# First-layer steps on the scores' PSUM banks: one slot in four, and two banks by turns after the last attention unit

## Chip, cores, metric

One core of a Trainium2 chip. The metric is the device time of one execution in microseconds (us). Before the change it is 310.82 us, the median of 3 runs (310.35 to 310.94).

## What is computed

The reference is sliding-window attention followed by a two-layer network with an ELU between the layers:

```python
# q, k, v: 8 batches, 8 heads, 576 positions, 64 wide
scores = scale * np.matmul(q, k.transpose(0, 1, 3, 2))
mask = (rel >= 0) & (rel < 128)
scores = np.where(mask, scores + bias[None], -1000000000.0)
attn = softmax(scores)                    # along the keys
x = matmul(attn, v)                       # -> 4608 tokens x 512
h = x @ w_in                              # 512 -> 2048
g = np.where(h > 0.0, h, np.exp(np.minimum(h, 0.0)) - 1.0)
out = g @ w_out                           # 2048 -> 512
```

## The kernel before

Everything runs in one hand-written order (the scheduler is off). The order is a list of numbered **slots**. In each slot the kernel issues, in this order: early tasks, one **first-layer step** (`hidden`, L297), the ELU of the step of the slot before (`done`, L531, which calls `elu`, L319), the slot's other tasks, its second-layer products (`product`, L384), and late tasks. Each engine takes its instructions in the order in which they were issued, so a wait in one of them holds back all that stands behind it on that engine.

**A first-layer step.** For a token block `t` of 512 tokens a step makes two chunks of 128 hidden units for 256 tokens, in one PSUM bank of 128 x 512 float32. TensorE runs 8 matmuls of 256 columns (L305; 16 shorter ones where the ring of transposed tokens wraps). ScalarE then reads the bank. In "soft" slots it does both parts of the exponential itself (L312, L313); in the others it does one pass (L315) and GpSimd clamps (L316). VectorE makes the ELU from that and from the bank (L323); this is the bank's last reader. A step is free to overwrite a bank when the ELU that read it last has ended. There are 16 steps for each block; blocks 2 to 8 have slots 38 to 149.

**PSUM.** The kernel uses all eight banks: `spa` (two banks, which are `sp[0]` and `sp[1]`), `sp[2]`, `sp[3]`, `hp[0]`, `hp[1]`, `av` and `op`. From slot 38 on, first-layer steps alternate between `hp[0]` and `hp[1]`, so a step reuses the bank of the step two slots earlier. The products of the second layer use `av` and `op`. For n = 17, the last half block, they use `sp[0]`, `sp[2]` and `sp[3]` instead, from slot 150 on.

**Attention.** Batches 2 to 7 start at the slots 31, 48, 66, 83, 100 and 117 (`START`). A batch has four units of four slots. A unit that starts at slot a does this:

- late in slot a: scores (L225) into `sp[0..3]`, 16 matmuls (32 in the last unit), in turn over the four banks, each on a quarter of the array's rows;
- slot a+1: ScalarE's exp of `spa` (L233), ahead of that slot's first-layer step; then weighing on VectorE (L241);
- slot a+2: ScalarE's exps of `sp[2]` and `sp[3]` (L236), again ahead of the step; then weighing;
- slot a+3: `all_values` (L263): value products into `spa` (L271), then reciprocal and division on VectorE (L276, L277), and a transposing DMA on SP's queue;
- the last unit only, slot a+4: `values` (L243) for the remaining 64 queries, 8 matmuls into `sp[2]` and then 8 into `sp[3]` (L253), with their reciprocals and divisions (L259, L260).

Scores of the next unit are issued late in slot a+4, so `sp[2]` and `sp[3]` have no user between the exps of slot a+2 and those scores (or those last value products). Slot numbers grow by four from unit to unit, and the last scores of batch 7 are in slot 129; its last value products are in slot 133.

**The second layer** computes pairs of 128 x 256 quarters with seven products in place of eight (lines 341 to 418). Its sums of slices of `g` and its combinations run on VectorE (L354) between the ELUs, and its copies on ScalarE (L396, L398). Seven 8-matmul products (L393) are spread over eight slots, so a slot without attention work is 8 first-layer and 7 second-layer matmuls.

The lines that give each step its bank:

```python
BUF = [hp[0], hp[1], sp[2], sp[3]]
for t in range(2, NTB):
    for j in range(16):
        step = (256 * (j // 8), 256, 2 * (j % 8), 2)
        HID[16 * t + 6 + j] = [(t, *step, BUF[(j + 1) % 2])]
```

Of the kernel before, what the change touches and what calls it, by code (L numbers as in the profile page):

```python
# [18 lines left out]
def kernel(  # L19
# [14 lines left out]
    NTB = NTOK // 512  # L34
# [42 lines left out]
    sp = [spa[:, 0, :], spa[:, 1, :]] + [ps_s.tile([128, 512], F32, name=f"sp{i}", tag=f"sp{i}") for i in (2, 3)]  # L77
    hp = [ps_h.tile([128, 512], F32, name=f"hp{i}", tag=f"hp{i}") for i in range(2)]
# [70 lines left out]
    with tc.manual_schedule():  # L149
# [341 lines left out]
        early, tasks, late, HID, OUT = {}, {}, {}, {}, {}  # L491

        def at(s, f, *a):
            tasks.setdefault(s, []).append((f, a))
# [4 lines left out]
        def after(s, f, *a):  # L499
            late.setdefault(s, []).append((f, a))  # L500
# [4 lines left out]
        BUF = [hp[0], hp[1], sp[2], sp[3]]  # L505
# [6 lines left out]
        steps += [(1, c0, 128, 4 * f, 4) for c0 in (256, 384) for f in range(4)]  # L512
        for s, step in enumerate(steps):
            HID[s if s < 18 else s + 6] = [(*step, (hp[0], hp[1], av, hp[1])[s] if s < 4 else BUF[(s + 1) % (3 if s < 18 else 2)])]
        for t in range(2, NTB):
            for j in range(16):
                step = (256 * (j // 8), 256, 2 * (j % 8), 2)
                HID[16 * t + 6 + j] = [(t, *step, BUF[(j + 1) % 2])]
        SEVEN = range(1, 18)

        XY = {1: (op, sp[3]), 2: (op, av)}
# [2 lines left out]
        for o in range(16 * NTB):  # L524
            t, ts, f = o // 16, o // 4 % 4, o % 4
            if o // 8 in SEVEN:
                continue
            s = (9, 11, 13, 14)[o] if o < 4 else 11 + o if o < 13 else 2 * o - 1 if o < 16 else 15 + o
# [62 lines left out]
        at(31, values, 1, 4, 1)  # L591
        at(32, turn, 1, 4)


        START = [None, None, 31, 48, 66, 83, 100, 117]

        TURN = [None, None, (22, 24, 25, 28), (35, 39, 43, 47)]
        REST = 32, 33, 36, 37
        for b in range(2, B):
            for u in range(4):  # L600
                a = START[b] + 4 * u
                after(a, scores, b, u)
# [6 lines left out]
                if u == 3:  # L609
                    at(a + 4, values, b, 4, 0, sp[2])  # L610
                    at(a + 4, values, b, 4, 1, sp[3])
                    at(a + 4, turn, b, 4)
            a = START[b - 1] if b > 2 else 0
            for n in range(4):
# [16 lines left out]
        for n in SEVEN:  # L631
            s = 15 + 8 * n
# [66 lines left out]
```

The softmax here doesn't subtract the row's maximum and nothing guards it: scores larger than these inputs give would overflow.

## Time and profile before

| | |
|---|---|
| Timed runs, median of 3 | 310.82 us (310.35 to 310.94) |
| Profiled execution, first to last instruction | 308.9 us |
| Granted TensorE clock, mean | 0.998 |
| Busy: TensorE matmul / VectorE / ScalarE / GpSimd | 300.1 / 257.5 / 241.8 / 108.4 us |
| L305, first-layer matmuls into hp | 1488, busy 144.2 us |
| L323, ELU, 128 x 512 | 679 ns each |
| L312 + L313, soft step on ScalarE | 597 + 631 ns each |
| L225, scores of batches 2 to 7 | first at 71.3 us, last at 264.5 us |

A row of the profile's groups names the line, the engine, the operation, what it writes and reads, the shape and the count; then the busy time, the mean of one in ns, and the idle time of the engine ahead of it with its releaser. In the timeline a row gives the start and the length in us of one instruction, or of a run of like ones ("x8"). TensorE's matmuls are pipelined, and their ends are modelled: rows of one run overlap, so an idle time between two ends says less than the distance between two starts.

Two views serve for what follows: the page, and the timeline of all engines in a few microseconds. The first-layer step of a slot is found in the timeline as a run of L305 on TensorE; its ELU is the L323 that belongs to it in order.

### The profile page before, as it was taken

To read this page: it belongs to the slowest core of one execution; us is meant where nothing else is said; L and a number is where in the kernel's file an instruction comes from. 1 tells how busy PE (TensorE), PEld (TensorE's weight loads), DVE (VectorE), ACT (ScalarE), POOL (GpSimd) and SP (SyncE) were. 2 spreads that over 40 slices of the span, in tenths; PEclk is the share of its full clock that TensorE was granted. 3 is DMA by queue.
4 is the path that set the end of the run, shared out by engine and by line. 5 is a ranking of instruction groups with operands and counts; after the bars stand their busy time and mean duration, and the time that the engine had idled before them with its cause. 6 is when DMAs were issued, how large, how long until landed. Compare 5 with 4: busy or idle time off the path is not lost.

```text
span 308.9 us, 9820 instructions
## 1 busy us (share of the span) xinstructions
PE 300.1 (97%) x4071; PEld 256.1 (83%) x4071; DVE 257.5 (83%) x498; ACT 241.8 (78%) x446; POOL 108.4 (35%) x163
## 2 busy tenths in 40 slices
PE   6899999999999999999999999999999999999995
PEld 4788875798888888988888888888899888898884
DVE  4646888988989998997989998989998788886782
ACT  4576678678798788878887889778888897968871
POOL 8937867273252315141616061706000001010000
PEclk9999999999999999999999999999999999999999
DMA  9999999999194919395969896999530202030103
GB/s 96 196 197 202 201 180 185 94 118 115 21 165 63 169 35 161 43 152 59 132 70 138 110 102 78 138 124 122 60 94 7 91 17 87 19 98 0 70 28 110
DMA packets 96509, 32.04 MB, mean 104 GB/s; under 512 B 83920, under 2 KB 91984, under 8 KB 96464
## 3 DMA queue, kind: packets, MB, share of 16 engines
q0 software_dynamic: 75920, 18.36, 64.2%
q1 hardware_dynamic: 20400, 12.98, 17.1%
q8 instruction: 32, 0.52, 0.7%
q14 instruction: 13, 0.11, 0.1%
q10 hardware_dynamic: 144, 0.07, 0.1%
HBM read 36.70 MB, written 9.44 MB: 149 GB/s over the span
## 4 chain that ended last, share of the span: by engine, by line
PE 72%; DVE 8%; DMA 6%; ACT 5%; POOL 4%; issue 4%; POOLq 0%; DVEq 0%
PE hp L305 33%; PE op L393 13%; PE av L393 12%; DMA VP<-in_v_dram 4%; PE spa L225 3%; PE spa L271 3%; DVE g L323 3%; POOL e L316 2%; PE sp L393 2%; ACT e L315 2%; DMA s<-in_q_dram 2%; ACT EX L236 1%; PE sp L253 1%; POOL VP L114 1%; DVE xn L260 1%
## 5 line engine op out<-in xcount | busy, mean ns | idle before, releaser
L305 PE MATMUL hp<-xT,wi 128*128 128x256 f16 (+3 forms) x1488 | 144.2, 245 | 1.0 <-DVE g L323 0.5
L305 PEld LDWEIGHTS <-wi 128*128 128x128 f16 x1600 | 119.9, 98 | 18.1 <-issue 6.3
L323 DVE SCALAR_TENSOR_TENSOR g<-e,hp 128x512 f16<-128x512 f32 x138 | 93.7, 679 | 22.2 <-ACT e L313 12.5
L316 POOL TENSOR_SCALAR e<-e 128x512 f32<-128x512 f32 x44 | 28.0, 636 | 158.8 <-ACT e L315 152.9
L312 ACT ACTIVATE e<-hp 128x512 f32<-128x512 f32 x98 | 58.6, 597 | 28.5 <-PE hp L305 23.1
L313 ACT ACTIVATE e<-e 128x512 f32<-128x512 f32 x100 | 63.1, 631 | 3.2
L393 PEld LDWEIGHTS <-S 128*128 128x128 f16 x544 | 51.2, 98 | 6.7 <-issue 0.6
L393 PEld LDWEIGHTS <-g 128*128 128x128 f16 x408 | 38.2, 98 | 4.7 <-issue 0.6
L241 DVE TENSOR_TENSOR EX<-EX,TAB 128x1024 f16<-128x1024 f16 x48 | 32.9, 686 | 6.2 <-ACT EX L236 4.0
L114 POOL DMA_DIRECT2D VP<-in_v_dram x40 | 34.6, 878 | 0.6 <-PE hp L305 0.3
L315 ACT ACTIVATE e<-hp 128x512 f32<-128x512 f32 x40 | 24.1, 601 | 10.9 <-PE hp L305 10.9
L393 PE MATMUL op<-T,S 128*128 128x256 f16 x200 | 30.0, 273 | 0.1
L233 ACT ACTIVATE EX<-spa 128x1024 f16<-128x1024 f32 x24 | 24.6, 1025 | 3.7 <-PE spa L225 3.4
L393 PE MATMUL av<-T,S 128*128 128x256 f16 x176 | 26.4, 273 | 0.1
L236 ACT ACTIVATE EX<-sp 128x512 f16<-128x512 f32 x48 | 26.0, 596 | 0.0
L354 DVE TENSOR_TENSOR S<-g 128x1024 f16<-128x1024 f16 (+2 forms) x35 | 23.5, 671 | 0.8 <-PE op L393 0.2
L393 PE MATMUL op<-wo,g 128*128 128x256 f16 x128 | 19.2, 272 | 0.1
L393 PE MATMUL av<-wo,g 128*128 128x256 f16 x120 | 18.0, 272 | 0.0
L277 DVE TENSOR_TENSOR xn<-spa,rden 128x512 f16<-128x512 f32 x24 | 16.6, 692 | 0.8
L108 POOL DMA_DIRECT2D st<-in_k_dram x24 | 16.2, 686 | 2.8 <-DMA s<-in_q_dram 1.9
L108 POOL DMA_DIRECT2D st<-in_q_dram x24 | 15.9, 666 | 0.6 <-DMA VP<-in_v_dram 0.6
L271 PE MATMUL spa<-VP,EX 128*128 128x65 f16 x336 | 15.4, 193 | 0.1
(139 smaller groups left out, 379.3 us busy)
## 6 DMA issues: line engine op xcount, KB each, us to landing
out_dram<-ob SPq DMA_DIRECT2D x35, 256.0 KB, 2.2
VP<-in_v_dram POOLq DMA_DIRECT2D x32, 128.0 KB, 5.7
st<-in_k_dram POOLq DMA_DIRECT2D x24, 144.0 KB, 5.2
st<-in_q_dram POOLq DMA_DIRECT2D x24, 144.0 KB, 5.9
wi<-in_moe_w_in_dram POOLq DMA_DIRECT2D x4, 512.0 KB, 10.7
wo<-in_moe_w_out_dram POOLq DMA_DIRECT2D x4, 512.0 KB, 10.1
VP<-in_v_dram POOLq DMA_DIRECT2D x8, 64.0 KB, 5.8
s<-in_k_dram POOLq DMA_DIRECT2D x1, 512.0 KB, 12.1
```

The costliest lines, as they stand in the source:

```text
L108: nc.gpsimd.dma_start(st[b][32 * g:32 * g + 32, w, :, :, :, :].rearrange("p h n j d -> p (h n) (j d)"), (q, k)[w][b, 2 * g:2 * g + 2, :, : ...
L114: nc.gpsimd.dma_start(VP[b % 2][0:p, n, :, 0:D], v[b, :, 128 * n:128 * n + p, :].rearrange("h p d -> p h d"))
L236: nc.scalar.activation(unit(b, u)[:, g, :, :], sp[g].rearrange("p (h c) -> p h c", h=2), AF.Exp, scale=0.125)
L241: V.tensor_tensor(out=e, in0=e, in1=TAB[:, int(u == 3), 2 * gp:2 * gp + 2, :, :], op=ALU.mult)
L271: nc.tensor.matmul(a[:, h // 4, h % 4, :], ex_[u][:, c:c + 128], VP[b % 2][:, n, h, 0:D + 1], start=j == 0, stop=j == len(parts) - 1)
L305: nc.tensor.matmul(p[:, l * w + u0:l * w + u1], w_in_sb[:, c, fc * 128:(fc + 1) * 128], xT[:, c, x0:x0 + u1 - u0], start=(c == 0), stop=(c ...
L312: nc.scalar.activation(e[:, 0:n], p[:, 0:n], AF.Relu, scale=-1.0)
L313: nc.scalar.activation(e[:, 0:n], e[:, 0:n], AF.Exp, scale=-1.0)
L315: nc.scalar.activation(e[:, 0:n], p[:, 0:n], AF.Exp)
L316: nc.gpsimd.tensor_scalar(out=e[:, 0:n], in0=e[:, 0:n], scalar1=1.0, scalar2=0.0, op0=ALU.min, op1=ALU.max)
L323: V.scalar_tensor_tensor(out=gs[t][:, f0:f0 + nf, c0:c0 + w], in0=sh(es.pop((t, c0, f0))), scalar=1.0, in1=sh(hps.pop((t, c0, f0))), op0=A ...
L393: nc.tensor.matmul(o, a[:, j, :], b[:, j, :], start=j == 0 and i in (1, 2, 5), stop=j == 7, skip_group_check=True)
```

## The change

From slot 38 to 145, first-layer steps no longer all use the two hp banks. In the slot a+3 of each unit of batches 2 to 7 the step's bank is `sp[2]` for the first three units of a batch and `sp[3]` for the fourth. After slot 133 (`ended` is 134) the odd slots use `sp[3]` and `sp[2]` by turns. All other steps take the hp banks by turns, counted over those steps alone. No instruction is added, removed or moved on any engine; the banks, and the waits that follow from them, differ. The list `START` is moved up in the file, so the lines after it have other numbers in the changed kernel.

```diff
+        START = [None, None, 31, 48, 66, 83, 100, 117]
+        spare = {a + 4 * u + 3: sp[2 + u // 3] for a in START[2:] for u in range(4)}
+        ended, full = START[-1] + 17, 0
         for t in range(2, NTB):
             for j in range(16):
+                s = 16 * t + 6 + j
                 step = (256 * (j // 8), 256, 2 * (j % 8), 2)
-                HID[16 * t + 6 + j] = [(t, *step, BUF[(j + 1) % 2])]
+                if s in spare and s < 16 * NTB + 2:
+                    bank = spare[s]
+                elif s >= ended and s < 16 * NTB + 2 and s % 2:
+                    bank = sp[2 + s // 2 % 2]
+                else:
+                    bank, full = hp[(full + 1) % 2], full + 1
+                HID[s] = [(t, *step, bank)]
```

More of the change, by code (lines that the diff above doesn't have):

```diff
@@ L592 @@
         at(32, turn, 1, 4)
-        START = [None, None, 31, 48, 66, 83, 100, 117]
         TURN = [None, None, (22, 24, 25, 28), (35, 39, 43, 47)]
```

## The prediction

> **What bounds the kernel now.** I read the page first (busy shares, chain, groups), then TensorE's own waits, then the timeline, all engines, around one attention unit and around the end of one batch.
>
> ```profile
> PE 300.1 (97%) x4071; PEld 256.1 (83%) x4071; DVE 257.5 (83%) x498; ACT 241.8 (78%) x446; POOL 108.4 (35%) x163
> ...
> PE 72%; DVE 8%; DMA 6%; ACT 5%; POOL 4%; issue 4%; POOLq 0%; DVEq 0%
> ...
> L305 PE MATMUL hp<-xT,wi 128*128 128x256 f16 (+3 forms) x1488 | 144.2, 245 | 1.0 <-DVE g L323 0.5
> ```
>
> TensorE carries 97% of the span and 72% of the chain. The third line books only 0.5 us of waiting for the ELU (L323) to the first layer, but that is idle time between modelled ends, which overlap (245 ns per row). Waits shorter than that show only in the starts. So I went through TensorE's rows by start: a 256-column matmul follows the one before it by 0.109 us (280.44 to 282.08 us holds 15 of them: 1.64), a 65-column one by 0.031. A start later than that is a stall.
>
> The timeline of the last batch (b = 7, third unit) shows both the wait that the change removes and the one that it adds:
>
> ```profile
> 260.09 1.04 PE L305 MATMUL hp<-xT,wi 128*128 128x256 f16 x8
> ...
> 261.55 0.82 PE L393 MATMUL av<-wo,g 128*128 128x256 f16 x6
> 261.57 0.69 DVE L323 SCALAR_TENSOR_TENSOR g<-e,hp 128x512 f16<-128x512 f32 x1 [0.46 <-ACT e L313]
> ...
> 262.18 0.68 DVE L354 TENSOR_TENSOR S<-S,g 128x1024 f16<-128x1024 f16 x1
> 262.31 1.03 PE L305 MATMUL hp<-xT,wi 128*128 128x256 f16 x8
> ...
> 262.78 0.20 DVE L276 RECIPROCAL rden<-spa 128x8 f32<-128x8 f32 x1
> 263.01 0.69 DVE L277 TENSOR_TENSOR xn<-spa,rden 128x512 f16<-128x512 f32 x1
> ...
> 263.62 0.68 DVE L323 SCALAR_TENSOR_TENSOR g<-e,hp 128x512 f16<-128x512 f32 x1
> ...
> 264.04 0.26 PE L225 MATMUL spa<-QT,KT 32*128 32x192 f16 x2
> 264.05 0.26 PE L225 MATMUL sp<-QT,KT 32*128 32x192 f16 x2
> ```
>
> Slot 129's step (262.31) could have started at 261.55 + 6 x 0.109 = 262.21. Its bank is free when the ELU of step 127 ends (261.57 + 0.69 = 262.26). It starts 0.05 after that, so 0.10 is lost; the 0.05 is the same in every such wait.
>
> **Part 1: the waits removed.** In the slots that the change touches (38 to 149) thirteen steps start late for this reason, in us: slot 43 0.13, 46 0.11, 49 0.09, 50 0.23, 70 0.35, 78 0.23, 91 0.13, 94 0.12, 99 0.13, 121 0.24, 125 0.11, 129 0.10, 133 0.11: 2.06 in all. That is the most this part can give. (Another 0.09 at each first step after scores is the change between row shapes and stays.) With one step of four on a scores bank, two of the three steps on hp reuse a bank three slots old and one still two slots old; 49 and 50 are of the latter kind, so 1.74 is removed directly.
>
> **Part 2: two banks by turns from slot 135 on.** The steps from 134 to 149 follow each other by 1.64 us, 15 matmuls x 0.109, with stalls of 0.001 to 0.002: nothing to win. A release that now comes 0.22 us early (2 slots old) will come 3.5 early. Value 0.
>
> **Part 3: the waits added.** No instruction moves on any queue, SP's and POOL's included; only banks and waits differ. A borrowed bank has two new edges. First, the borrowed step (slot a+3 of a unit that starts at slot a) waits for that unit's exp (L236). Second, whoever writes the bank next waits for the borrowed step's ELU: the next unit's scores at the end of slot a+4 for sp[2], and the second half of the batch's last value product (L253) in slot a+16 for sp[3]. Behind the waiting matmul stands all of TensorE's queue: the rest of the scores, hence ScalarE's exps and VectorE's weighing, and the next first-layer step.
>
> In the rows above, step 128's ELU runs 263.62 to 264.30. Scores began at 264.04; they can now write sp[2] only at 264.30 + 0.05 = 264.35: +0.31 against before. The 0.10 saved at slot 129 doesn't lower that, as nothing on the way to this ELU depends on step 129. It is the end of a run on VectorE without a gap: ELU of 127, S, reciprocal, xn, ELU of 128, that is 261.57 to 264.30, started by ScalarE (L313 ends 261.54), which itself worked since the unit's scores. So it is a loop: scores, exps, two ELUs with xn between, scores again. The loop is now longer than TensorE's work between two scores (7.80 us from 256.24 to 264.04, less the stalls), and it repeats after each unit, so the losses add up.
>
> The same sum (ELU end + 0.05 - scores' start, against before, so with part 1 contained) for each unit after the first of a batch: slot 39 +0.03, 43 +0.30, 52 +0.08, 60 +0.13, 70 +0.04 (0.35 saved, 0.39 waited), 78 +0.04, 87 +0.30, 91 +0.30, 95 +0.10, 108 +0.20, 121 +0.31, 125 -0.11 (ELU early enough, the saving stays), 129 +0.31; nothing at 56, 74, 104, 112. Sum **+2.03**.
>
> The end of a batch is worse. Here batch 5's, slot 99:
>
> ```profile
> 203.34 0.68 DVE L354 TENSOR_TENSOR S<-g 128x1024 f16<-128x1024 f16 x1
> 203.47 1.03 PE L305 MATMUL hp<-xT,wi 128*128 128x256 f16 x8
> ...
> 204.18 0.69 DVE L277 TENSOR_TENSOR xn<-spa,rden 128x512 f16<-128x512 f32 x1
> ...
> 204.34 0.65 PE L253 MATMUL sp<-VP,EX 128*128 128x65 f16 x16
> ...
> 204.78 0.68 DVE L323 SCALAR_TENSOR_TENSOR g<-e,hp 128x512 f16<-128x512 f32 x1
> ```
>
> The 16 value matmuls come straight after the step; the last eight (from 204.34 + 8 x 0.031 = 204.59) go to sp[3], which step 98's ELU leaves at 205.46: released at 205.51, +0.92. In slots 47, 64, 82, 99, 116, 133: +0.72, 0.23, 0.49, 0.92, 0.74, 0.41. Sum **+3.51**.
>
> The wait for the exp is late four times only, at slots 81, 98, 115, 132 (0.09, 0.40, 0.11, 0.35). Each stands ahead of a batch end whose ELU is held by VectorE's queue, not by this step, so it is contained in that sum: +0. After slot 47 TensorE is 0.72 late while VectorE is busy without a gap to past slot 50, so the waits at 49 and 50 vanish: **-0.32**.
>
> Costs without an edge: reading another bank. L315 takes 597 ns from sp and 597 to 620 from hp, L323 686 from either: 0. The built program has 43 fewer second waits on ScalarE (17 ns a row), 5 fewer on TensorE (51 ns), 9 more on POOL (17 ns): between -0.99 and +0.15; I take 0, since most of these rows lie ahead of a wait that lasts longer, and keep the ends.
>
> **Sum.** 2.03 + 3.51 - 0.32 = +5.22 on the span: 308.9 to 314.1. The profiled execution has 308.9 from first to last instruction; the median of the timed runs is 310.82, 1.9 above. I add to the median: **316.0 us**, 1.7% slower.
>
> The Trainium skill's "Perfetto Trace Analysis", section "Matmul Optimizations", asks that all eight PSUM banks be leveraged for parallelism, which speaks for the change; by it the 2.06 us would be won and nothing paid. The rows differ, since sp[2] is not a spare bank in slot a+4: scores want it back 0.31 us before its reader ends.
>
> **Rivals.**
> *Faster, 308.8 us (6%).* The 2.06 us go and the ELU of a borrowed step is never late. That decides at the lag from the step's last matmul to its ELU's end: for step 120 it is 3.17 us (245.52 to 248.69), and scores, freed of the stall at 121, would be ready 2.7 after that matmul (248.43 - 0.24). For it: without queueing the lag is 2.02 (slots 134 to 148). Against: xn and S stand ahead of that ELU in VectorE's fixed order.
> *Only the batch ends hurt, 312.6 us (10%).* If VectorE catches up in each stall and the next scores never wait, part 3's 2.03 turns into the 1.40 saved at slots 43, 70, 78, 91, 94, 121, 125, 129: 3.51 - 1.40 - 0.32 = +1.79. For it: a late TensorE gives VectorE time, as at slot 49. Against: VectorE idles until ScalarE in each unit (0.46 above), so it has no backlog to work off.
> *The borrowed step's own delay passes on, 317.4 us (12%).* If the 0.95 of late exps do push their ELUs, and the savings of 0.32 and 0.11 don't come: +6.60.
> *No change within 0.2% (4%)*: the bank isn't what those steps wait for, and VectorE's order hides the rest.
>
> **How the numbers follow.** Forecast 316.0 with 68%. What a measurement of this kernel can tell from no change is about 0.2% (0.6 us). Slower by more: 68 + 10 + 12 = 90%; same 4%; faster 6%. The range takes in both slower rivals and the -0.99 of the second waits only in part: 312.4 to 317.6.
>
> **What would show it.** Right: scores in slots 43, 87, 91, 121, 129 start 0.05 after an L323 that reads sp; the eight last L253 matmuls start apart from the eight first by 0.5 to 0.9 us; no stall at slots 70, 78, 121; slots 134 to 149 still 1.64 apart. Wrong: scores that start without waiting, or batch ends whose value products still run 16 in a row.

## The result, and the profile after

| | before | after |
|---|---|---|
| Timed runs, median of 4 | 310.88 us (310.35 to 311.23) | 315.75 us (315.09 to 316.19) |
| Ratio, 95% interval | | 1.0158 (1.014 to 1.0175) |
| First to last instruction, profiled | 308.9 us | 314.4 us |

The change makes the kernel 1.6% slower, 4.9 us by the ratio. The forecast was 316.0.

The page of the changed kernel, the same three lines as before:

```profile
PE 302.4 (96%) x4071; PEld 257.6 (82%) x4071; DVE 258.8 (82%) x498; ACT 243.4 (77%) x446; POOL 107.9 (34%) x163
...
PE 59%; DVE 13%; ACT 9%; DMA 9%; issue 5%; POOL 5%; POOLq 0%; DVEq 0%; ACTq 0%
...
L305 PE MATMUL hp<-xT,wi 128*128 128x256 f16 (+3 forms) x1224 | 114.1, 242 | 0.6 <-DVE g L323 0.5
```

Each engine does the same work (4071 matmuls; busy times within 2.3 us), but TensorE's part of the chain falls from 72% to 59%, while VectorE's grows from 8% to 13% and ScalarE's from 5% to 9%: where TensorE ran alone it now waits for them. (Not all of the shift is that: DMA's part grew from 6% to 9%, since one load of keys, 88.37 to 95.05 us, lies on the chain after and none did before.) TensorE's own waits name whom for (us in total, times, longest):

```profile
PE sp L253 <- DVE g L323: 1.7, 4, 0.5
...
PE sp L225 <- DVE g L323: 0.6, 3, 0.3
...
PE sp L305 <- ACT EX L236: 0.4, 2, 0.3
```

None of these three rows existed before. They are too small, for the reason given for such rows above: they count only what lies between modelled ends. Starts give the size. Here are the rows of slots 128 and 129, the ones that the prediction worked with:

```profile
264.89 1.04 PE L305 MATMUL sp<-xT,wi 128*128 128x256 f16 x8
...
266.36 0.82 PE L393 MATMUL av<-wo,g 128*128 128x256 f16 x6
266.38 0.69 DVE L323 SCALAR_TENSOR_TENSOR g<-e,hp 128x512 f16<-128x512 f32 x1 [0.46 <-ACT e L313]
...
267.01 1.04 PE L305 MATMUL hp<-xT,wi 128*128 128x256 f16 x8
...
268.43 0.68 DVE L323 SCALAR_TENSOR_TENSOR g<-e,sp 128x512 f16<-128x512 f32 x1
...
268.75 0.26 PE L225 MATMUL spa<-QT,KT 32*128 32x192 f16 x2
...
269.17 0.26 PE L225 MATMUL sp<-QT,KT 32*128 32x192 f16 x2 [0.16 <-DVE g L323]
```

Slot 129's step starts at 267.01 = 266.36 + 6 x 0.109: its stall is gone. The scores' first two matmuls start at 268.75, and the third, on sp[2], only at 269.17, which is 268.43 + 0.68 + 0.06, the end of the ELU that reads sp. Before, the four banks started within 0.01 us. The idle note says 0.16; the starts say 0.42.

The end of batch 5:

```profile
204.35 1.03 PE L305 MATMUL sp<-xT,wi 128*128 128x256 f16 x8 [0.25 <-ACT EX L236]
...
206.47 1.04 PE L305 MATMUL hp<-xT,wi 128*128 128x256 f16 x8
...
206.92 0.69 DVE L277 TENSOR_TENSOR xn<-spa,rden 128x512 f16<-128x512 f32 x1
...
207.34 0.41 PE L253 MATMUL sp<-VP,EX 128*128 128x65 f16 x8
207.53 0.68 DVE L323 SCALAR_TENSOR_TENSOR g<-e,sp 128x512 f16<-128x512 f32 x1
...
208.26 0.40 PE L253 MATMUL sp<-VP,EX 128*128 128x65 f16 x8 [0.52 <-DVE g L323]
```

The 16 value matmuls, one run before, are two runs of eight, 0.92 us apart instead of 0.25. The second starts 0.05 after 207.53 + 0.68. The first row is the borrowed step of slot 98: it starts 0.05 after the exp of sp[3] has ended (204.30), 0.42 later than TensorE could have started it.

To see every place at once, take the start of each first-layer step against the same step before. The distance changes only where something is won or lost:

| what | predicted, us | read in the starts, us |
|---|---|---|
| scores, slots 39, 43, 52, 60 | 0.03, 0.30, 0.08, 0.13 | 0.03, 0.33, 0.32, 0.14 |
| scores, slots 70, 78, 87, 91, 95 | 0.04, 0.04, 0.30, 0.30, 0.10 | 0.04, 0.05, 0.30, 0.32, -0.08 |
| scores, slots 108, 121, 125, 129 | 0.20, 0.31, -0.11, 0.31 | 0.19, 0.31, -0.10, 0.31 |
| batch ends, slots 47, 64, 82, 99, 116, 133 | 0.72, 0.23, 0.49, 0.92, 0.74, 0.41 | 0.56, 0.23, 0.49, 0.94, 0.76, 0.40 |
| slots 49 and 50 | -0.32 | -0.30 |
| slots 134 to 149 | 0 | 0.00 |
| sum | 5.22 | 5.24 by these rows, 5.18 as a whole |

Another 0.34 us of the two spans' difference stands already at slot 30, ahead of the first changed step, where the two executions waited differently for their first loads. The profiled execution of the changed kernel, 316.19 us, is the slowest of its four; the medians are 4.9 apart.

### The profile page after: what moved, and what is told of

Read it like the earlier page. It is cut to its first block, busy times and chain, and to the rows that moved or that the text cites. A ratio compares the mean times of both kernels' runs of the same rounds, so it can differ in the third digit from the quotient of the medians.

```text
span 314.4 us, 9790 instructions
## 1 busy us (share of the span) xinstructions
PE 302.4 (96%) x4071; PEld 257.6 (82%) x4071; DVE 258.8 (82%) x498; ACT 243.4 (77%) x446; POOL 107.9 (34%) x163
## 4 chain that ended last, share of the span: by engine, by line
PE 59%; DVE 13%; ACT 9%; DMA 9%; issue 5%; POOL 5%; POOLq 0%; DVEq 0%; ACTq 0%
PE hp L305 21%; PE op L393 10%; PE av L393 10%; PE sp L305 6%; DVE g L323 5%; DMA VP<-in_v_dram 5%; ACT EX L236 3%; PE spa L225 2%; DMA st<-in_k_dram 2%; ACT e L315 2%; PE spa L271 2%; POOL st L108 2%; POOL e L316 2%; DMA s<-in_q_dram 2%; PE sp L225 2%
## 5 line engine op out<-in xcount | busy, mean ns | idle before, releaser
L305 PE MATMUL hp<-xT,wi 128*128 128x256 f16 (+3 forms) x1224 | 114.1, 242 | 0.6 <-DVE g L323 0.5
L323 DVE SCALAR_TENSOR_TENSOR g<-e,hp 128x512 f16<-128x512 f32 x109 | 74.0, 679 | 21.4 <-ACT e L313 11.4
L312 ACT ACTIVATE e<-hp 128x512 f32<-128x512 f32 x73 | 43.7, 599 | 24.0 <-PE hp L305 19.9
L305 PE MATMUL sp<-xT,wi 128*128 128x256 f16 (+3 forms) x360 | 35.5, 246 | 0.4 <-ACT EX L236 0.4
L315 ACT ACTIVATE e<-hp 128x512 f32<-128x512 f32 x36 | 21.7, 602 | 10.9 <-PE hp L305 10.7
L323 DVE SCALAR_TENSOR_TENSOR g<-e,sp 128x512 f16<-128x512 f32 x34 | 23.2, 681 | 3.8 <-ACT e L313 3.0
L312 ACT ACTIVATE e<-sp 128x512 f32<-128x512 f32 x27 | 16.1, 596 | 5.6 <-PE sp L305 4.5
```

What stands on the lines that cost most here:

```text
L305: nc.tensor.matmul(p[:, l * w + u0:l * w + u1], w_in_sb[:, c, fc * 128:(fc + 1) * 128], xT[:, c, x0:x0 + u1 - u0], start=(c == 0), stop=(c ...
L312: nc.scalar.activation(e[:, 0:n], p[:, 0:n], AF.Relu, scale=-1.0)
L315: nc.scalar.activation(e[:, 0:n], p[:, 0:n], AF.Exp)
L323: V.scalar_tensor_tensor(out=gs[t][:, f0:f0 + nf, c0:c0 + w], in0=sh(es.pop((t, c0, f0))), scalar=1.0, in1=sh(hps.pop((t, c0, f0))), op0=A ...
```

## The experiments

The theory: the cost is the wait for a borrowed bank's ELU by those who want the bank back, the next scores (2.1 us) and a batch's last value product (3.4). The rivals: the borrowed steps' own wait for the exps; a bank that is slower to use; an ELU that TensorE or ScalarE makes late, not VectorE's order. Each run's distance from before is given twice: as the ratio of the timed runs, and as what the steps' starts gain or lose between slot 30 and slot 149 ("starts"), which for the changed kernel is +5.18.

**One part at a time.**

```diff
# e1_sp2_alone: range(4) -> range(3) in `spare`, and nothing by turns
# e2_sp3_alone: range(4) -> range(3, 4), and nothing by turns
# e3_turns_alone
+        spare = {}
```

> Only the first three units of a batch lend sp[2]; the fourth lends nothing, and no banks by turns at the end. If the cost is the wait of the next scores for the borrowed step's ELU: about +1.9 us against before (2.1 read in the changed kernel's starts, less some 0.2 because without the batch-end stalls the two waits at slots 49 and 50 come back and the scores of slot 52 wait less), so about 312.8. If the cost were the wait of borrowed steps for the exps, which was late only in slots that use sp[3]: no change, 310.9.

312.19 us; ratio to before 1.0041 (1.0015 to 1.0067), some 1.3 us; starts +1.80. The scores' waits cost by themselves, and they add up: the distance grows by about 0.3 us at each of slots 43, 87, 91, 121 and 129. The exps as the cause are out: none was late here.

> Only the fourth unit of a batch lends sp[3]. If the last value products wait for the borrowed step's ELU: about +3.4 us at the six batch ends less 0.3 at slots 49 and 50, +3.1 in all, about 314.0. If only the late exps cost (0.98 us in the changed kernel): 311.9.

314.25 us; ratio 1.0103 (1.0047 to 1.016); starts +3.18. The batch ends cost 3 us alone, and e1 and e2 together (4.98) come near the 5.18.

> Only the two banks by turns from slot 135 on. Both theories: no change, 310.9, with steps 1.64 us apart as before. If a stall between steps was hidden by the pipelining of the rows, it would be faster by some tenths of a us.

310.40 us; ratio 0.9985 (0.9961 to 1.001); starts -0.02. Nothing. In the changed kernel the same slots, on sp by turns, still follow each other by 1.64 us:

```profile
284.32 1.04 PE L305 MATMUL hp<-xT,wi 128*128 128x256 f16 x8
...
285.96 1.04 PE L305 MATMUL sp<-xT,wi 128*128 128x256 f16 x8
...
287.60 0.60 PE L305 MATMUL hp<-xT,wi 128*128 128x256 f16 x4
```

(The last row shows four of its eight matmuls, since the view ends there.) The run also clears the bank itself: 8 matmuls into sp take what 8 into hp take.

**Who makes the ELU late.** The division of the fourth unit goes behind that slot's ELU:

```diff
-                at(a + 3, all_values, b, u)
-                at(a + 3, turn, b, u)
-                if u == 3:
+                at(a + 3, all_values, b, u, (0, 1) if u < 3 else (0,))
+                if u < 3:
+                    at(a + 3, turn, b, u)
+                else:
+                    at(a + 4, all_values, b, u, (1,))
+                    at(a + 4, turn, b, u)
```

(Part 0 of `all_values` is its matmuls, part 1 its reciprocal and division.)

> The changed kernel, with the reciprocal and division of a batch's fourth unit (0.83 us on VectorE) issued behind the borrowed step's ELU instead of ahead of it. If VectorE's order makes that ELU late: it ends up to 0.83 us earlier, the six waits of the last value products (0.67, 0.24, 0.41, 0.68, 0.64, 0.16, together 2.8 us) go to about 0, and the time falls from 315.75 to about 313.0. If ScalarE or TensorE sets that ELU's time: no change, 315.7.

313.64 us; ratio 1.0092 (1.0061 to 1.0123), against the changed kernel's 1.0158; starts +3.02, so 2.2 of the 2.8 us are back. Batch 5's end in this kernel (L326 is the ELU here, L357 a sum, L280 the division):

```profile
204.95 0.69 DVE L357 TENSOR_TENSOR S<-g 128x1024 f16<-128x1024 f16 x1
...
205.57 0.69 DVE L326 SCALAR_TENSOR_TENSOR g<-e,sp 128x512 f16<-128x512 f32 x1
...
206.20 0.65 PE L253 MATMUL sp<-VP,EX 128*128 128x65 f16 x16
...
207.02 0.69 DVE L280 TENSOR_TENSOR xn<-spa,rden 128x512 f16<-128x512 f32 x1
```

The ELU follows S directly, and the 16 value matmuls are one run again. VectorE's order made it late there. At five of the six batch ends the ELU now starts 0.4 to 0.8 us earlier against the step behind it. At the sixth, slot 133, it does not move:

```profile
272.94 0.61 POOL L319 TENSOR_SCALAR e<-e 128x512 f32<-128x512 f32 x1 [13.63 <-ACT e L318]
...
273.06 1.04 PE L308 MATMUL hp<-xT,wi 128*128 128x256 f16 x8
...
273.58 0.69 DVE L326 SCALAR_TENSOR_TENSOR g<-e,sp 128x512 f16<-128x512 f32 x1 [0.82 <-POOL e L319]
```

The ELU starts 0.53 after step 133 (273.06 to 273.58), as in the changed kernel (275.50 to 276.03), because GpSimd's clamp ends just ahead of it in both (in the changed kernel at 275.99, the division at 276.04): there the borrowed step's own late exp and the passes behind it are as late as VectorE's order. The slot loses 0.40 either way. What did not come back of the 2.8: 0.15 at slot 133 and 0.06 at slot 82; 0.20 more at the scores of slot 87, where GpSimd's clamp of step 86 took 0.86 us and not 0.64; 0.18 at step 66, which starts 0.05 after the end of the ELU two steps before; and the waits at slots 49 and 50 return (0.28), against 0.25 less at the scores of slot 52. The late exps (0.08, 0.41, 0.12, 0.36) stand in the starts as they did in the changed kernel.

**Which instruction waits.** Two edits change who stands at the bank. The second leaves out the scores that go to sp[2], and its exp of that group reads sp[3] in place of sp[2], so its results are not those of the reference:

```diff
# e5_swap_halves
-                    at(a + 4, values, b, 4, 0, sp[2])
-                    at(a + 4, values, b, 4, 1, sp[3])
+                    at(a + 4, values, b, 4, 0, sp[3])
+                    at(a + 4, values, b, 4, 1, sp[2])
# e6_no_scores_sp2
-                        for g in range(4):
+                        for g in (0, 1, 3):
```

> The changed kernel, with the two halves of a batch's last value product on each other's bank: the first 8 matmuls go to sp[3], the last 8 to sp[2]. If they wait for the ELU of the step that borrowed sp[3]: now all 16 stand behind it, 0.245 us more at each of six batch ends, +1.5 us, about 317.2. If the halves wait for something of their own (their weights, or the xn buffers): no change, 315.7.

317.44 us; ratio 1.0208 (1.0186 to 1.0229); starts +6.63, 1.45 more than the changed kernel where 1.47 was expected. All 16 matmuls now stand behind the ELU:

```profile
208.58 0.68 DVE L323 SCALAR_TENSOR_TENSOR g<-e,sp 128x512 f16<-128x512 f32 x1
...
209.31 0.64 PE L253 MATMUL sp<-VP,EX 128*128 128x65 f16 x16 [0.76 <-DVE g L323]
```

> The changed kernel without the scores that go to sp[2] (a quarter of the heads of batches 2 to 7 is not computed; the exp of that group reads sp[3] instead, so ScalarE's work is the same, and TensorE's too, since the four banks' score matmuls run side by side). If the scores' cost is their wait for the ELU that reads sp[2]: that wait is gone while every step still has its borrowed bank; the gross waits read in the starts are 3.5 us, so about 312.3. If the lateness comes from elsewhere (exps, VectorE reading sp): no change, 315.7.

312.71 us; ratio 1.0063 (1.0041 to 1.0084); starts +2.16, 3.0 back of the 3.5 expected. The scores that are left out took TensorE no time of their own: slots 56, 104 and 112, which wait for nothing in either kernel, take as long without them. The borrowed step's ELU still ends after the scores start, and nobody minds:

```profile
265.73 0.68 DVE L323 SCALAR_TENSOR_TENSOR g<-e,sp 128x512 f16<-128x512 f32 x1
...
266.05 0.26 PE L225 MATMUL spa<-QT,KT 32*128 32x192 f16 x2
266.05 0.25 PE L225 MATMUL sp<-QT,KT 32*128 32x192 f16 x1
```

Most of the 0.5 that did not come is read in the starts: small losses ahead of the steps 45, 72, 80 and 93 (0.04 to 0.16 each, 0.35 together), whose cause I did not follow, and 0.88 lost at the batch end of slot 47 where the changed kernel loses 0.67.

**Work in place of the wait.** The last value product goes behind its slot's seven second-layer matmuls (`at` -> `after` in its three lines):

> The changed kernel, with a batch's last value product issued behind the seven second-layer matmuls of its slot (0.76 us) instead of ahead of them. If TensorE merely stands at that product until the ELU ends: useful work fills the wait, and 2.8 us of it go but for little, about 313.0. If the ELU itself is pushed later by what TensorE does meanwhile: little change, about 315.5.

313.28 us; ratio 1.0078 (1.0058 to 1.0097); starts +2.56, 2.6 back. The ELU was not pushed (at each of the six ends it starts as long after the step behind it as in the changed kernel, 0.53 to 1.06 us); TensorE had merely stood there.

That VectorE's order is what makes the ELU late is tested at the batch ends alone. For the scores it rests on the rows, where VectorE runs without a gap up to that ELU; no run moved a division there.

**Tries for a faster kernel.** e8: `spare = {a + 15: sp[2] for a in START[2:]}`, no turns, the halves swapped, and the late division. e9: the same lending and slot 124, no turns, the halves swapped, the late value product. e10: the kernel before with the late value product alone.

> A try for a faster kernel than both: only the fourth unit of a batch lends a bank, sp[2] (whose exp ends about 0.5 us before sp[3]'s), the division of that unit stands behind the borrowed step's ELU, and the half of the last value product that uses sp[2] comes last. If the two theories of the batch end hold (late exp of sp[3], ELU behind the division), no wait is left there and the stalls before at slots 46, 99 and 133 (0.34 us together) go: about 310.5 against 310.9. If the scores or the values still wait: above 310.9.

312.04 us; ratio 1.0039 (1.0024 to 1.0053); starts +1.38. A miss by 1.5 us or more. The value matmuls still waited at four batch ends, 0.13 to 0.51 us: without the division ahead of it the ELU of step 132 ran 271.74 to 272.42, straight behind GpSimd's clamp (271.09, 0.61), and the last eight were ready at 271.97. There ScalarE and GpSimd alone make the borrowed step late enough. At slots 82 and 116 its ELU starts 0.03 to 0.04 after ScalarE's second pass has ended; at slot 99 a sum of VectorE (S) still stands ahead of it. And three first-layer steps (66, 86 and 135) came 0.16 to 0.20 late, each 0.05 after the end of the ELU two steps before.

> A second try: only the fourth unit of a batch lends a bank (sp[2], early exp), the last value product stands behind its slot's seven second-layer matmuls, so that the ELU has 0.76 us more, and slot 124, the one place where the scores did not wait, borrows too. If the waits are only a matter of how late the bank is wanted back: none is left, the stalls at 46, 99, 125 and 133 (0.45 us together) go, and some 0.1 comes back at slot 66: about 310.3 against 310.6. If the late value product holds something else up (its xn, the next scores): above 310.6.

311.07 us; ratio 1.0013 (1.0001 to 1.0025); starts +0.55. Not faster. The value product still waited at slot 99, though it stood behind the second-layer work (0.28 us lost; it starts again 0.05 after the ELU of step 98), and step 46 lost 0.14 to a wait that the profile puts to the DMA of its transposed tokens, not to a bank.

> The kernel before with the last value product of a batch moved behind its slot's second-layer matmuls and nothing borrowed: the control of the run beside it and of the one with late values. No bank wait is touched, so no change but for 0.1 at slot 66: 310.6 to 310.8. If that move alone is worth something, 0.3 or more below.

310.95 us; ratio 1.0013 (0.9994 to 1.0031); starts +0.59, a little worse than expected. The profile of e10 shows the place, slot 135, which e9 shares (0.46 in both):

```profile
272.72 0.42 DVE L260 TENSOR_TENSOR xn<-sp,rden 64x256 f16<-64x256 f32 x1
...
273.39 0.67 DVE L323 SCALAR_TENSOR_TENSOR g<-e,hp 128x512 f16<-128x512 f32 x1
...
274.11 1.03 PE L305 MATMUL hp<-xT,wi 128*128 128x256 f16 x8 [0.30 <-DVE g L323]
```

The later value product pushes its own divisions (L260) back on VectorE, the ELU of step 133 stands behind them, and step 135 waits for that ELU. That, too, is a bank wanted before its ELU has ended. No version here beats the kernel before; one that borrowed only at slot 124 could win 0.1 us, under what can be measured, and wasn't tried.

## Why the prediction was right

- **What bounds the kernel, and the gain of at most 2.06 us.** Right: the eleven stalls said to be removed directly are gone in the starts (1.73 us; the prediction's thirteen items add up to 2.08, not 2.06), and no step from slot 38 on starts late for a bank on hp; what is left there are the 0.09 us behind scores.
- **The scores' waits, +2.03.** Read: +2.16 in the starts; e1 has them without the rest of the change, and in e6 they are gone with the instruction that waited.
- **The batch ends, +3.51.** Read: +3.38; e2, e5 and e7 move them as that step of the sum requires, and e4 does at five of the six. That the late exps are contained in them is read in the totals: slots 98 and 99 lose 0.94, slots 115 and 116 0.76, where 0.92 and 0.74 were forecast without the exps and 0.40 and 0.11 would have come on top. One reason was too strong: at slot 133 the ELU is not held by VectorE's queue alone. The step's own late exp gives the same 0.40 there, as e4 shows, so that term came out right with half of its cause.
- **-0.32 at slots 49 and 50.** The waits vanished as said (-0.30), but 0.24 of it was given back two slots later, where the scores of slot 52 lost 0.32 and not 0.08. The prediction kept the old end for the ELU of step 51; it came later, since ScalarE's and VectorE's run to it starts with the scores of slot 48, which had moved with TensorE.
- **Two single terms were off by 0.16 to 0.18** and nearly cancel that: slot 47 (0.56, not 0.72) and slot 95 (-0.08, not +0.10), where GpSimd's clamp ahead of that run took 0.61 to 0.62 us instead of the 0.77 to 0.78 of the profile before; nothing in the sum foresaw that, so that 5.22 comes so near 5.18 is in part luck.
- **Turns at the end, 0.** Right (e3: no step moved).
- **The second waits saved on ScalarE and TensorE, taken as 0 of at most -0.99.** No distance in the table needs them. The profile's rows for such waits are 26 fewer on ScalarE, 4 fewer on TensorE and as many as before on GpSimd, not 43, 5 and 9 more; at 17 and 51 ns that is 0.65 us at most.
- **The rivals.** "Only the batch ends hurt" fails with e1. "The borrowed step's own delay passes on" fails with slots 98 and 99, where the 0.42 of the late exp and the batch end together come to 0.94, as if the exp cost nothing. For "faster", the lag of step 120 would have had to be 2.7 us; it is 3.18 after, 3.17 before.

The Trainium skill asks that all eight PSUM banks be leveraged ("Perfetto Trace Analysis", "Matmul Optimizations"). Taken as a reason to spread the steps over more banks, it would have promised a gain here. All eight were in use before and after; the measurement decides, and what counted was when each was wanted back.

## What to carry to other kernels

A buffer that looks free between two users is free only if the borrower's last reader ends before the second user wants it. Compare that gap with the borrower's whole lag from the last write to the end of the last read, here 2.0 us without queueing and up to 3.2 with it, against gaps, in the kernel before, of 2.2 to 2.4 at the batch ends and 2.6 to 3.1 at the scores. A stall that is removed in a loop gives nothing if another wait of the same loop closes later: add each removed stall and each new wait at the place where they meet, and take the later of the two, not their sum. And when an instruction is moved to fill a wait on one engine, see what its dependants push back on another engine's queue (slot 135 in e9 and e10).

## What the runs showed of the hardware

A wait of TensorE for a semaphore of VectorE or ScalarE ended 0.05 to 0.06 us after the releaser's recorded end in all rows used here. Matmuls on a quarter of the rows each, on four banks, start within 0.01 us of each other, and the order still holds: the one on sp[2] that waited held back those behind it on the other banks (268.75 to 269.17).
